# Moving the v copies to ACT, merging the substitution groups and changing two priorities in a scan-and-MLP kernel

## The chip, the cores and the metric

One core of a Trainium2 chip runs the whole program. The metric is device time in microseconds (us) of one launch; lower is better. A run is measured several times and the median is given.

## What is computed

The reference is a recurrence over 768 time steps (4 batches, 8 heads, head size 40) and then two MLPs over the 3072 resulting rows of 320 numbers:

```python
for t in range(S):
    y[:, :, t] = np.einsum('bhd,bhde->bhe', rt, state)
    Sa = np.einsum('bhde,bhe->bhd', state, at)
    state_decay = state * wt[:, :, None, :] - np.einsum('bhd,bhe->bhde', Sa, bt)
    state = state_decay + np.einsum('bhd,bhe->bhde', vt, kt)
...
h = x @ w_in                                    # 320 -> 2048
x = (np.maximum(h, 0) + alpha * np.minimum(h, 0)) @ w_out
g = x @ w_gate                                  # 320 -> 1536
out = (g / (1 + np.exp(-g)) * (x @ w_val)) @ w_out2
```

The weights come in as 64-bit floats and are narrowed on the chip.

## The kernel before, in words

**Blocks and items.** Time is cut into six blocks of 128 steps (`m` = 0 to 5), each of two chunks of 64. A block has four items, one for each batch, so there are 24. For each block the kernel does three things. `preps` builds, item by item, decay products by scans on DVE (`prep_a`, L502 and L509), the operand `AN` (L519), the operand `kbt` (L531), its products on PE (L543), copies of these on ACT into the block's triangular matrix `TT[m % 2]` (L549, L552) and into `AN` (L556, with a triangular select on POOL, L557), and transposed keys `KB` (L571, L574). `inverse(m)` inverts that matrix for all four items together. `seq` then carries the state through the two chunks of one item.

**The inverse.** The matrix is a 2x2 arrangement of 32x32 triangles. A DVE transpose (L589) brings the triangles into the scratch tile `ml`, and POOL writes an identity into `tl` (L591, L592). Then 31 substitution steps run on DVE: step `kk` multiplies the column `kk` of `ml` by the row `kk` of `tl` (L604) and subtracts the product from the rows below (L612). The columns of `tl` are cut into groups by `cuts`. For block 0 the cuts are 0, 16, 32 (`CL0`). For every later block they are 0, 10, 32 (`CUT`, `C2`); the second group has work only from step 10 on, and its columns do not depend on those of the first. Two DVE transposes (L615, L617) and two rounds of small matmuls with ACT copies (L625 to L652) finish the inverse. From block 1 on the scratch tiles share the two buffers of `kbt` (`scr`, L583), so the next block's `kbt` comes after the inverse has let go of them.

**The scan.** `seq(i, ch)` runs item `i` in chain 0 or 1; the two chains interleave. For each chunk `enter_chunk` takes one of two `gs` buffers: DVE writes the decayed state into one half of its partitions (L685, two instructions) and POOL decays the state itself (L685, POOL). Two POOL copies of 64 partitions by 160 elements put the rows of `v` in the other half (L699), after which `load_v` fetches the v of a later item. Then PE transposes the state (L707) and ACT copies it to `s0` (L709); PE multiplies (`zp`, L714), ACT copies (`zs`, L716), PE applies the inverse (`pp`, L724), ACT copies and negates (L726, L728, L734), PE forms `gp` (L741), DVE masks it (L744), PE forms `yp` (L756, L760), and DVE updates the state (L764) and scales the result (L768). The `yp` matmuls at L756 are the last readers of a `gs` buffer. The result goes to memory from ACT's queue (L776).

**The MLPs.** `mlp1(j)` runs block `j` of the first MLP in 16 steps `f`: 8 matmuls up (`up_mm`, L238), a leaky ReLU on ACT and DVE (L277, L278), a split into two parts (ACT L184, DVE L185), and 8 matmuls down. Its tiles take the places that the preparation of blocks 0 and 1 used, and its input is the scan's result. For block 0 its first eight steps run on the two halves of the batches one after the other. The second MLP runs at the end, after all scans.

**The conversion.** `conv1` narrows the first MLP's weights, 32 tiles in all: loads on SP's queue into two `raw` buffers, three DVE instructions (L172 to L174), one on ACT (L175), one more on DVE (L177), a copy on ACT (L184), a subtraction on POOL (L185), and a store on SP's queue.

**What sets the order.** The kernel is traced by `drive`, which advances several generators in proportion to their progress; each instruction gets a running number. A planner then orders each engine's queue: of the instructions that are ready it takes the one with the lowest number, and `drive` lowers the numbers of a generator by the amount given with it. While block 0 is scanned these amounts are as follows. `seq(0)`, `seq(1)`, and behind them `seq(2)` and `seq(3)`, have `SP` = 3000. `rest1`, which is the rest of block 1's preparation and then `inverse(1)`, has `HP2`. The conversion has `CP`. `mlp1(0)` has `MP` = 0. `CP` is also that of four conversions traced beside `inverse(0)`, which has 3000. From block 1 on scans, preparation and inverse all have 3000 and the MLP has 0. The conversion also carries an explicit edge (`behind`, L808): its DVE instructions come behind the latest step of the inverse that was traced before them. `rest1` is traced in 67 steps, 27 of preparation and 40 of `inverse(1)`, beside 26 conversions.

```python
drive(
    (seq(0, 0), N_SEQ, SP), (seq(1, 1), N_SEQ, SP),
    (take(rest1, int(nrest * RA)) if RA < 1 else rest1, FAC * nrest, HP2),
    (take(c1, NC1), NC1 - EC - EC0, CP),
)
```

Of the kernel before, what the change touches and what calls it, by code (L numbers as in the profile page):

```python
# [42 lines left out]
CL0 = (0, 16, 32)  # L43
# [1 line left out]
RA = 1.0  # L45
MP = 0
YB = 1
CP = 2000
HP2 = 3000
XI = 1  # L50
IB = 8
WB = 4
PRI = 3000
WCB = 2
GSB = 2
CUT = 0
C2 = 10
GPB = 2
DEP = 1
HOLD = 10  # L60
# [3 lines left out]
HALF = 32  # L64
# [4 lines left out]
def kernel(  # L69
# [15 lines left out]
    nc = tc.nc  # L85
# [34 lines left out]
    def drive(*gens, lead=0, engs=0, lag=1, who=0):  # L120
        live = [[*g, 0, j] for j, g in enumerate(gens)]
        names = ["PE", "DVE", "Activation", "Pool"]
        while live:
            e = min(live, key=lambda e: e[3] / e[1])
            try:
                tc.cur_priority -= e[2]
                with ExitStack() as st:
                    if e[4] >= lead and who >> (e[4] - lead) & 1:
                        for b in range(4):
                            log = crit.get(b, [])  # L130
                            if engs >> b & 1 and len(log) >= lag:
                                st.enter_context(tc.issue_after(log[-lag]))
                    n0 = len(traced())
                    ok = next(e[0], 0)
                    if e[4] < lead:
                        new = traced()[n0:]
                        for b in range(4):
                            mine = [x for x in new if str(x.engine).split(".")[-1] == names[b]]
                            if mine:
                                crit.setdefault(b, []).append(mine[-1])  # L140
                tc.cur_priority += e[2]
                e[3] += 1
                if ok == 0:
                    live.remove(e)
            except StopIteration:
                tc.cur_priority += e[2]
                live.remove(e)

    def chain(*gens):
        for g in gens:  # L150
            yield from g
# [427 lines left out]
    def scr(m, j):  # L579
        if m == 0:  # L580
            return bp.tile([128, HALF * HALF], F32, tag=f"la{j}", name="la")
        if ALIAS:
            return kbt_p.tile([128, HALF * HALF], F32, tag="kbt", name="la")  # L583
        return mac_p.tile([128, HALF * HALF], F32, tag=f"la{j}", name="la")

    def inverse(m):
        mc = tt = TT[m % 2]
        ml = scr(m, 0).rearrange("p (a b) -> p a b", a=HALF)
        nc.vector.transpose(out=ml, in_=mc[:, :, 0:HALF].rearrange("p n t -> p t n"))  # L589
        tl = scr(m, 1).rearrange("p (a b) -> p a b", a=HALF)  # L590
        nc.gpsimd.memset(tl, 0.0)  # L591
        nc.gpsimd.memset(tl.rearrange("p a b -> p (a b)")[:, 0:HALF * HALF:HALF + 1], 1.0)  # L592
        yield
        cuts = (CUT, C2, HALF) if m else CL0
        for kk in range(HALF - 1):
            tvs = []
            for c0, c1 in zip(cuts, cuts[1:]):
                nr, ns = HALF - 1 - kk, min(kk + 1, c1) - c0
                if ns <= 0:
                    continue  # L600
                most = max((HALF - 1 - q) * (min(q + 1, c1) - c0) for q in range(HALF))
                tmp = (mac_p if m else bp).tile([128, most], F32, tag=f"tmp{c0}", name="tmp")
                tv = tmp[:, 0:nr * ns].rearrange("p (a b) -> p a b", a=nr)
                nc.vector.tensor_tensor(  # L604
                    out=tv,
                    in0=ml[:, kk + 1:HALF, kk:kk + 1].to_broadcast([128, nr, ns]),
                    in1=tl[:, kk:kk + 1, c0:c0 + ns].to_broadcast([128, nr, ns]),
                    op=ALU.mult,
                )
                tvs.append((tv, tl[:, kk + 1:HALF, c0:c0 + ns]))  # L610
            for tv, dst in tvs:
                mark["inv"] = nc.vector.tensor_tensor(out=dst, in0=dst, in1=tv, op=ALU.subtract)  # L612
            yield
        tn = scr(m, 0).rearrange("p (a b) -> p a b", a=NG)
        nc.vector.transpose(out=tn.rearrange("p n s -> p s n"), in_=tl.rearrange("p t s -> p s t"))  # L615
        yield
        mark["inv"] = nc.vector.transpose(out=tt[:, :, 0:HALF].rearrange("p n t -> p t n"), in_=tl)  # L617
        yield
        es = scr(m, 1).rearrange("p (a b) -> p a b", a=NG)
        NH = NG // 2  # L620
        for g in range(2):
            eps = (ps_b if m else bps).tile([128, NH, HALF], F32, tag="b" if m else f"s{2 + g}", name="eps")
            for n in range(NH):
                for q in (0, 2):
                    nc.tensor.matmul(  # L625
                        eps[32 * q + 32:32 * q + 64, n, :],
                        mc[32 * q:32 * q + 32, g * NH + n, HALF:L],
                        tn[32 * q:32 * q + 32, g * NH + n, :],
                        tile_position=(32 * q, 32 * q + 32),
                    )  # L630
            for q in (1, 3):
                pr = slice(32 * q, 32 * q + 32)
                nc.scalar.copy(out=es[pr, g * NH:g * NH + NH], in_=eps[pr])
            yield
        for q in (1, 3):
            pr = slice(32 * q, 32 * q + 32)
            nc.scalar.copy(out=tt[pr, :, HALF:L], in_=tt[pr, :, 0:HALF])
            nc.gpsimd.memset(tt[pr, :, 0:HALF], 0.0)
            yield
        for g in range(2):  # L640
            dps = (ps_b if m else bps).tile([128, NH, HALF], F32, tag="b" if m else f"s{2 + g}", name="dps")
            for n in range(NH):
                for q in (1, 3):
                    nc.tensor.matmul(
                        dps[32 * q - 32:32 * q, n, :],
                        es[32 * q:32 * q + 32, g * NH + n, :],
                        tt[32 * q:32 * q + 32, g * NH + n, HALF:L],
                        tile_position=(32 * q, 32 * q - 32),
                    )
            for q in (0, 2):  # L650
                pr = slice(32 * q, 32 * q + 32)
                nc.scalar.mul(out=tt[pr, g * NH:g * NH + NH, HALF:L], in_=dps[pr], mul=-1.0)  # L652
            yield
# [7 lines left out]
    def seq(i, ch, own=None):  # L661
        m, bb = order[i]
# [32 lines left out]
        for c in range(CPB):  # L695
            cs = slice(c * L, c * L + L)
            gs = nxt
            for h, pr in ((0, hi), (1, lo)):
                nc.gpsimd.tensor_copy(  # L699
                    out=gs[pr, h::2, :, L:L + D],  # L700
                    in_=rv.rearrange("t (q j d) -> t q j d", j=2, d=D)[(lo, hi)[c], h::2],
                )
# [98 lines left out]
    def after(ins, g):  # L801
        while True:
            with tc.issue_after(ins.ins):
                if next(g, 0) == 0:
                    return
            yield

    def behind(g):  # L808
        while True:
            with tc.issue_after(mark["inv"].ins) if "inv" in mark else nullcontext():  # L810
                if next(g, 0) == 0:
                    return
            yield
# [10 lines left out]
    def take(g, n):  # L824
        for _ in range(n):
            if next(g, 0) == 0:
                return
            yield
# [8 lines left out]
    c1 = after(mark["prep"], c1)  # L837
    p1, c1 = behind(p1), behind(c1)
    drive((inverse(0), N_INV, HP), (take(p1, EP), EP + .1, BP), (take(c1, EC), EC + .1, CP), lead=1, engs=G0, lag=LG0, who=W0)
    p1, c1 = after(mark["inv"], p1), after(mark["inv"], c1)  # L840
    rest1 = chain(p1, inverse(1))
    nrest = B * N_PREP - EP + N_INV
    if FA == 0:
        drive(
            *((chain(seq(j, j), seq(j + 2, j)), 2 * N_SEQ, SP) for j in range(2)),
            (rest1, FAC * nrest, HP2),
            (take(c1, NC1), NC1 - EC - EC0, CP),
            lead=2, engs=G1, lag=LG1, who=W1,
        )
    else:  # L850
# [5 lines that stand above are left out]
# [9 lines left out]
    if FA:  # L865
        drive(
            (seq(2, 0), N_SEQ, SP), (seq(3, 1), N_SEQ, SP),
            (rest1, FAC * nrest * (1 - RA) + .1, HP2),
            (take(gms[0], 2 * FA + 1), 2 * FA + 1, MP),
        )  # L870
# [160 lines left out]
```

## Time and profile before

| what | value |
|---|---|
| median of 3 runs | 1250.2 us (1249.28 to 1252.76) |
| the profiled execution | 1245.15 us, its span 1243.4 us |
| mean granted TensorE clock in it | 0.949 of full speed |
| DVE / ACT / POOL busy | 781.3 us (63%) / 592.6 us (48%) / 312.6 us (25%) |
| end of `inverse(0)` and `inverse(1)`, last ACT instruction | 95.9 us, 205.9 us |
| last state update of the scans | 748 us |

All positions in the trace are in us from the start of the span. The profiled execution took 5 us less than the median of the runs, and 1.75 us of it lie outside its span. PE, PEld, DVE, ACT, POOL and SP are TensorE's matmuls, its weight loads, VectorE, ScalarE, GpSimd and the engine that issues most DMAs. Busy time is the union of an engine's instructions, so overlapping instructions are counted once; an instruction's duration runs from its start to its end even where the next one has started already.

### The profile page before, as it was taken

What the parts mean: (1) busy time and instruction counts of PE and PEld (TensorE: products, weight loads), DVE (VectorE), ACT (ScalarE), POOL (GpSimd) and SP (SyncE); (2) the same over time, 40 slices, a digit from 0 to 9 for tenths busy, and PEclk for the clock granted to TensorE, in tenths of its full rate; (3) what the DMA queues carried; (4) which work ended last, traced back from release to release, by engine and by line L of the source; (5) the groups of instructions that cost most, each with busy time, mean ns of one, the idle gap of its engine ahead of it and who ended that gap; (6) DMA issues with size and microseconds to landing.
All of it is one profiled execution on the core that took longest, in us unless ns stands there. A gap on an engine that the chain in (4) does not pass through costs nothing.

```text
span 1243.4 us, 24467 instructions
## 1 busy us (share of the span) xinstructions
PE 1095.8 (88%) x9056; PEld 928.7 (75%) x9056; DVE 781.3 (63%) x1689; ACT 592.6 (48%) x1463; POOL 312.6 (25%) x502
## 2 busy tenths in 40 slices
PE   3345787899799989989999899999999999999998
PEld 2244577777687777777777687888888888888887
DVE  7999999898669758974967444677732323232222
ACT  4547448844763674477455533455432323232222
POOL 9425443613121222252126300334500000000000
PEclk9658697999899999999999999999999999999999
DMA  5534577874545454464448648865210101000000
GB/s 149 168 115 133 180 257 251 263 228 126 161 127 176 134 161 142 144 196 145 145 139 266 201 131 292 283 213 153 73 47 1 47 1 38 1 22 1 22 1 22
DMA packets 92486, 166.36 MB, mean 134 GB/s; under 512 B 12752, under 2 KB 42704, under 8 KB 92368
## 3 DMA queue, kind: packets, MB, share of 16 engines
q1 hardware_dynamic: 84208, 160.87, 41.2%
q10 hardware_dynamic: 8160, 3.93, 1.1%
q8 instruction: 72, 1.18, 0.4%
q14 instruction: 46, 0.38, 0.1%
HBM read 136.98 MB, written 27.79 MB: 133 GB/s over the span
## 4 chain that ended last, share of the span: by engine, by line
PE 52%; DVE 20%; ACT 10%; DMA 8%; issue 6%; POOL 3%; SPq 1%; ACTq 0%; DVEq 0%; POOLq 0%
PE pg L238 10%; PE pv L238 10%; PE u L238 8%; PE o L952 3%; PE o L951 3%; PE o L953 3%; DVE la L612 3%; DVE tmp L604 3%; DMA raw_wa<-in_wa_dram 2%; PE gp L741 2%; PE d L243 2%; DMA xa<-xd 2%; PE d L244 2%; PE d L245 2%; DVE gs L685 2%
## 5 line engine op out<-in xcount | busy, mean ns | idle before, releaser
L184 ACT CAST gh<-g 128x512 fp32r<-128x512 f32 (+1 forms) x176 | 105.9, 602 | 175.2 <-DVE g L967 116.7
L967 DVE TENSOR_TENSOR g<-pv,sg 128x512 f32<-128x512 f32 x72 | 49.8, 691 | 200.1 <-PE pv L238 200.0
L185 DVE TENSOR_TENSOR gl<-g,gh 128x512 fp32r<-128x512 f32 (+1 forms) x176 | 119.5, 679 | 77.0 <-ACT gh L184 76.2
L238 PE MATMUL u<-xh,wt 128*128 128x512 f32 (+1 forms) x416 | 147.6, 397 | 15.9 <-DVE g L278 12.6
L278 DVE SCALAR_TENSOR_TENSOR g<-g,neg,u 128x512 f32<-128x512 f32 (+1 forms) x104 | 72.9, 701 | 63.0 <-ACT g L277 62.4
L238 PEld LDWEIGHTS u<-xh,wt 128*128 128x128 f32 x416 | 79.0, 193 | 34.9 <-DVE g L278 16.8
L238 PE MATMUL pg<-xh,w 128*128 128x512 f32 x288 | 102.0, 394 | 0.7 <-ACT sg L965 0.7
L965 ACT ACTIVATE sg<-pg 128x512 f32<-128x512 f32 x72 | 43.0, 597 | 124.3 <-PE pg L238 124.3
L238 PE MATMUL pv<-xh,w 128*128 128x512 f32 x288 | 100.5, 389 | 0.0
L277 ACT ACTIVATE g<-u 128x512 f32<-128x512 f32 (+1 forms) x104 | 58.7, 564 | 81.6 <-PE u L238 65.0
L543 PE MATMUL mnp<-AN,kbt 128*128 128x128 f32 x384 | 60.7, 311 | 32.1 <-POOL la L591 15.9
L952 PE MATMUL o<-w,gh 128*128 128x320 f32 x288 | 87.7, 309 | 0.0
L951 PE MATMUL o<-w,gh 128*128 128x320 f32 x288 | 87.1, 308 | 0.0
L244 PE MATMUL d<-gl,wt 128*128 128x512 f32 (+1 forms) x208 | 80.9, 391 | 1.2 <-DVE gl L185 1.2
L699 POOL COPY gs<-raw_v 64x160 f32<-64x160 f32 x96 | 42.3, 441 | 157.7 <-PE yp L756 70.1
L543 PEld LDWEIGHTS mnp<-AN,kbt 128*128 128x128 f32 x384 | 54.3, 219 | 36.2 <-POOL AN L517 17.6
L604 DVE TENSOR_TENSOR tmp<-la 128x96 f32<-128x96 f32 (+43 forms) x306 | 78.6, 281 | 3.2 <-POOL la L592 1.3
L238 PE MATMUL u<-xl,wt 128*128 128x512 f32 (+1 forms) x208 | 80.2, 386 | 0.2 <-DVE xl L185 0.2
L612 DVE TENSOR_TENSOR la<-la,tmp 128x96 f32<-128x96 f32 (+43 forms) x306 | 77.6, 278 | 1.9
L245 PE MATMUL d<-gh,wt 128*128 128x512 f32 (+1 forms) x208 | 78.5, 380 | 0.0
L557 POOL TENSOR_SCALAR_AFFINE_SELECT AN<-AN 64x256 f32<-64x256 f32 x96 | 48.5, 505 | 117.9 <-ACT AN L556 88.8
L953 PE MATMUL o<-w,gl 128*128 128x320 f32 x288 | 76.1, 309 | 0.0
(118 smaller groups left out, 2678.6 us busy)
## 6 DMA issues: line engine op xcount, KB each, us to landing
wt<-wd SPq DMA_DIRECT2D x98, 384.0 KB
wt<-wd SPq DMA_DIRECT2D x98, 320.0 KB
wd<-wc SPq DMA_DIRECT2D x24, 384.0 KB
raw<-in_moe_w_out_dram SPq DMA_DIRECT2D x28, 320.0 KB
raw_wa<-in_wa_dram SPq DMA_DIRECT2D x48, 160.0 KB
raw_bk<-in_bk_dram SPq DMA_DIRECT2D x48, 160.0 KB
wd<-wc SPq DMA_DIRECT2D x20, 320.0 KB
raw<-in_moe_w_in_dram SPq DMA_DIRECT2D x16, 256.0 KB
```

The costliest lines, as they stand in the source:

```text
L184: nc.scalar.copy(out=h, in_=raw)
L185: eng.tensor_tensor(out=l, in0=raw, in1=h.bitcast(F32), op=ALU.subtract)
L238: nc.tensor.matmul(ps, lt, rh, start=(i == 0), stop=(i == len(ops) - 1))
L244: nc.tensor.matmul(ps, wh, gl, start=False, stop=False)
L245: nc.tensor.matmul(ps, wl, gh, start=False, stop=last)
L278: nc.vector.scalar_tensor_tensor(g, g, neg[:, f:f + 1], ps, ALU.mult, ALU.add)
L543: nc.tensor.matmul(ps[:, s].rearrange("p h t -> p (h t)"), kbt[:, g * SH + s].rearrange("p j t -> p (j t)"), an[:, :, g * SH + s, :],)
L604: nc.vector.tensor_tensor(out=tv, in0=ml[:, kk + 1:HALF, kk:kk + 1].to_broadcast([128, nr, ns]), in1=tl[:, kk:kk + 1, c0:c0 + ns].to_broad ...
L612: mark["inv"] = nc.vector.tensor_tensor(out=dst, in0=dst, in1=tv, op=ALU.subtract)
L951: nc.tensor.matmul(ops[q], gh[:, ts], wh, start=first, stop=False)
L952: nc.tensor.matmul(ops[q], gh[:, ts], wl, start=False, stop=False)
L953: nc.tensor.matmul(ops[q], gl[:, ts], wh, start=False, stop=last)
```

## The change

The v copies go from `nc.gpsimd.tensor_copy` to `nc.scalar.copy`, with the same tiles and partitions. For blocks 1 to 5 the substitution has one group of columns instead of two. `CP` goes from 2000 to 3000 and `HP2` from 3000 to 1000.

```diff
-CP = 2000
-HP2 = 3000
+CP = 3000
+HP2 = 1000
...
-CUT = 0
-C2 = 10
...
-        cuts = (CUT, C2, HALF) if m else CL0
+        cuts = (0, HALF) if m else CL0
...
             for h, pr in ((0, hi), (1, lo)):
-                nc.gpsimd.tensor_copy(
+                nc.scalar.copy(
                     out=gs[pr, h::2, :, L:L + D],
                     in_=rv.rearrange("t (q j d) -> t q j d", j=2, d=D)[(lo, hi)[c], h::2],
                 )
```

## Rows read from the trace of the kernel before

**Rows 1.** The page's first part: busy time, share, instructions of PE.

```profile
PE 1095.8 (88%) x9056; PEld 928.7 (75%) x9056; DVE 781.3 (63%) x1689; ACT 592.6 (48%) x1463; POOL 312.6 (25%) x502
```

**Rows 2.** Busy time by stretch: length, PE, PEld, DVE, ACT, POOL, granted clock, DMA.

```profile
93.00:206.00 113.00, 81.25 (x997) 69.91 (x992) 106.35 (x270) 69.13 (x202) 48.96 (x76) 0.77 0.63 203
206.00:315.00 109.00, 97.27 (x1100) 83.83 (x1101) 96.36 (x235) 66.26 (x188) 39.97 (x68) 0.97 0.66 206
315.00:651.00 336.00, 307.90 (x3338) 252.50 (x3337) 246.16 (x614) 200.59 (x540) 88.73 (x168) 0.98 0.51 152
870.00:1243.00 373.00, 367.88 (x1905) 323.49 (x1903) 116.20 (x173) 104.98 (x187) 17.20 (x16) 1.00 0.07 23
```

**Rows 3.** The same view over the substitution of inverses 1 and 3.

```profile
118.00:191.00 73.00, 52.58 (x592) 44.85 (x594) 70.33 (x211) 33.95 (x105) 32.55 (x52) 0.79 0.66 213
...
357.00:413.00 56.00, 53.15 (x461) 42.18 (x461) 51.41 (x154) 23.35 (x62) 10.58 (x22) 1.00 0.53 158
```

**Rows 4.** Final transposes: inverse 1 (timeline of DVE), 2 and 3 (chain that ended last).

```profile
189.59 1.96 DVE L617 STREAM_TRANSPOSE tt<-la 128x1024 f32<-128x1024 f32 x1
...
299.56 2.00 DVE tt L617
...
411.16 1.99 DVE tt L617
```

**Rows 5.** Groups by line and form: substitution instructions of four sizes.

```profile
L612 DVE TENSOR_TENSOR la<-la,tmp 128x175 f32<-128x175 f32 x6 | 2.0, 333 | 0.0
...
L604 DVE TENSOR_TENSOR tmp<-la 128x10 f32<-128x10 f32 x5 | 0.8, 169 | 0.1
...
L604 DVE TENSOR_TENSOR tmp<-la 128x240 f32<-128x240 f32 x2 | 0.8, 399 | 0.0
...
L612 DVE TENSOR_TENSOR la<-la,tmp 128x63 f32<-128x63 f32 x2 | 0.4, 221 | 0.0
```

**Rows 6.** Timeline of DVE in inverse 0, two groups interleaved: start, length.

```profile
51.68 0.47 DVE L604 TENSOR_TENSOR tmp<-la 128x175 f32<-128x175 f32 x2
52.06 0.47 DVE L612 TENSOR_TENSOR la<-la,tmp 128x175 f32<-128x175 f32 x2
```

**Rows 7.** Timeline of DVE at the end of inverse 3, one group left.

```profile
407.16 0.19 DVE L604 TENSOR_TENSOR tmp<-la 128x30 f32<-128x30 f32 x1
407.38 0.19 DVE L612 TENSOR_TENSOR la<-la,tmp 128x30 f32<-128x30 f32 x1
```

**Rows 8.** The v copies: their group, their line, and who waited for them.

```profile
L699 POOL COPY gs<-raw_v 64x160 f32<-64x160 f32 x96 | 42.3, 441 | 157.7 <-PE yp L756 70.1 <-DVE tmp L604 46.6 <-DVE gl L185 17.3
...
L699 POOL COPY gs<-raw_v x96: 311/319/1166, 18.3 to 721.7; 64x160 f32<-64x160 f32 x96
...
  POOL wc L185: 1.0, 1
  PE sp L707: 0.3, 1
```

**Rows 9.** ACT copies by form: the same form from PSUM, a larger one from SBUF.

```profile
L734 ACT ACTIVATE gs<-pp 64x160 f32<-64x160 f32 x96 | 28.5, 297 | 5.4 <-PE pp L730 4.4
...
L676 ACT COPY pv<-raw_vt 128x256 f32<-128x256 f32 x48 | 17.2, 404 | 19.5 <-DMA xd<-pv 11.3 <-DMA raw_vt<-in_vt_dram 6.3 <-issue 1.6
```

**Rows 10.** Who waited: total us, times, longest; L764's wait; SP from 81 to 250.

```profile
POOL gs L699 <- PE yp L756: 70.1, 10, 20.2
...
  PE yp L760: 3.7, 5
...
SPq L210 <- POOL wc L185: 23.5, 12, 4.0
```

**Rows 11.** DVE readers of the raw weights (three for each conversion), 206 to 250 us: busy, instructions.

```profile
206.00:250.00 44.00, 13.57 (x21) 0.96 0.81 256
```

**Rows 12.** The conversion's fourth DVE instruction, by form.

```profile
L177 DVE SCALAR_TENSOR_TENSOR wz<-wz,wy 128x384 f32<-128x384 f32 x24 | 13.9, 580 | 4.2 <-ACT wz L175 3.9
```

## The prediction, made before the changed kernel had run

> **What bounds the kernel now.** I read the busy times first, then the stretches, then the parts that the change touches. PE is busy for 1095.8 of 1243.4 us [rows 1], so 148 us are PE's idle time, and only a smaller idle time (or a higher clock) can move the end: the matmuls themselves don't change. The stretches show where it lies [rows 2]. From 870 us on PE is idle for 5 of 373 us; nothing can be won there. From 93 to 206 it is idle for 32 of 113 us at a granted clock of 0.77, and DVE is busy for 106 of the 113: DVE binds. From 206 to 315 DVE has 96 of 109 us and PE 97: both bind. From 315 to 651 PE has 308 of 336 us (92%) and DVE 246 (73%): 28 us are left to win, and DVE time saved counts for about half, because PE is nearly full. I take that weight from these two shares; no row proves it.
>
> Within the later blocks DVE is again full while a substitution runs: 51.4 of 56 us in inverse 3 [rows 3], and inverses 2, 4 and 5 look the same. Preparation and inverse form a loop through the shared scratch buffers, and its period is steady: 299.56 to 411.16, 111.6 us between the last transposes of two inverses [rows 4].
>
> **One group instead of two, blocks 1 to 5.** Two groups take 31 + 21 = 52 pairs of instructions, one takes 31. So 42 instructions go from each inverse, 210 in all. The elements stay: the sum of (31 - kk)(kk + 1) over the steps is 5456 for each of the two lines. From 10 to 240 elements the duration grows from 169 to 399 ns, 1.0 ns an element, which leaves 159 ns fixed [rows 5]. But durations are not what DVE's time costs. In the interleaved groups a 175-element and a 63-element instruction last 333 + 221 = 554 ns [rows 5], while the next pair starts 0.38 us later [rows 6]: each starts some 85 ns before the one ahead ends. Where an instruction needs the result of the one just ahead, the start comes 0.22 us after a start of 0.19 us length [rows 7], 30 ns after its end. So the fixed part is about 75 ns when other work stands between, and 189 ns when not, 114 ns more.
>
> Before: 104 x 75 ns + 10.9 us of elements = 18.7 us, and 20 instructions of the last ten steps of the first group, which by then has no partner, at 114 ns more: 21.0 us. After: 62 x 75 ns + 10.9 = 15.6 us if other DVE work stands in every gap, 22.6 us if in none. The gain lies between 5.4 and -1.6 us for one inverse. Which end it is follows from how much other work there is: during inverse 1 DVE runs 211 instructions, 104 + 3 of them its own, so 104 others for 62 gaps [rows 3]; I take 5.0 us. During inverse 3 there are 154, so 47 others [rows 3], and they come in twos and threes; with 25 gaps filled, 37 x 114 ns remain and the gain is 1.2 us. Inverse 1 counts fully, inverse 2 nearly (1.0), the three later ones by half (1.8): **-7.8 us**.
>
> The rows contradict a rule that would make this part much larger. The Trainium skill (VectorE: DVE Perf Modes, The DRAIN you can't avoid) says that after each DVE instruction the next one waits until the pipeline has emptied, and that a semaphore between them adds nothing. By that rule each removed instruction gives back its whole fixed part; the starts in the rows contradict it for independent neighbours. What it would give is the second rival.
>
> **The copies.** POOL loses 96 x 441 ns = 42.3 us [rows 8]. Almost nothing waits for these copies: 1.0 us of a POOL instruction and 0.3 us of a transposition [rows 8]. So their going shortens no chain; the rest of the path from L764 to L709 (DVE, POOL's decay, PE) covers them, and it stays. What may be won is contention: the mean is 441 ns but the median 319 [rows 8], so something held the copies up for 96 x 122 ns = 11.7 us, and DVE may have been held as long. Between 0 and 11.7 us I take 4, a third of it before 315 us in full, two thirds by half: **-2.5 us**.
>
> ACT gains 96 copies of 64x160 from SBUF. The trace has that form only from PSUM, 297 ns, and a larger one from SBUF, 404 ns [rows 9]; I take 0.31 us, 30 us in all, 5 us a block of some 110. They must wait for the last reader of the `gs` buffer, `yp` at L756. POOL, with little else to do, waited 70.1 us for that; DVE, which waits for the end of the same group of matmuls at L764, 3.7 us [rows 10]. ACT is busy for 60% of the time from 93 to 651 [rows 2] and is like DVE in this; I take 3.7 us. Behind the waiting copies stand ACT's parts of the other chain, the MLP's ReLU and split, and the stores to memory at L776. For its own chain the copy lies where ACT has nothing to do. It delays others by 0.6 us a pair when ACT is busy: 48 x 0.6 x 0.6 = 17 us at worst, 0 at best, and as PE mostly has other matmuls queued I take 2.5 us net: **+2.5 us**. `load_v` on SP now follows ACT; its tile is for two items later, so nothing waits.
>
> **The priorities.** `inverse(1)` goes behind all four scans of block 0 and behind the conversion. The conversion can't run away from it: its edge holds it behind the inverse's steps, and by the proportional tracing 23 of the 26 conversions are traced before the substitution's last step. But it need no longer lag. Seven conversions run after 206 us now (21 readers in 13.57 us [rows 11], and 7 x about 0.55 us for the fourth instruction [rows 12]); less 28 overlaps of 85 ns that is 15 us of DVE. Three of the seven stay behind by the edge's count, so some 9 to 15 us of DVE work can come ahead of the end of inverse 1, and leave the stretch from 206 to 250, where DVE is nearly full. As long as DVE binds both stretches, order alone changes nothing: what inverse 1 loses the next block gets back. The scans of items 2 and 3 end earlier, so the second half of `mlp1(0)`'s input comes earlier, which can use some of PE's 32 idle us. Bounds: -6 (an estimate: a fifth of that idle time) and +15; I take **0**, the cover being that block 2's preparation and scan are freed of the same work. Without that cover it is the first rival. The conversion beside `inverse(0)` also rises, to the inverse's own priority: at most one more conversion, 2.2 us of DVE, falls inside; bounds 0 and +2.2, taken as 0 for the same reason. On SP's queue the conversions' loads and stores pass loads of block 1's raw tiles and weight fetches; their stores already held that queue for 23.5 us in 12 waits, 4.0 at most [rows 10]. Five more such waits early would be 10 us of SP's time, ahead of loads that are for an item or a step later; I take 0.
>
> **The sum.** -7.8 - 2.5 + 2.5 + 0 = -7.8 us. Against the profiled execution, 1245.15 us, that is 1237.3; that execution lies 5 us under the median of the runs, so for the median I say 1250.2 - 7.8 = **1242.4 us**.
>
> **Rivals.**
> - *Inverse 1 comes too late (slower).* For it: the loop's period was as long without conversions, 111.6 us [rows 4], as it was with seven of them (189.59 to 299.56, 110.0 [rows 4]), so freeing DVE of them may give nothing back. Price: at the upper bound all 15 us come before the end of inverse 1 and stay lost; less the 7.8, 1250.2 + 15 - 7.8 = 1257 us. It decides if the last transpose of inverse 1 ends after about 200 us and that of inverse 2 shifts as far. Against it: DVE was busy for 94% and 88% of the two stretches [rows 2], and in a full queue order gives back what it takes. 0.22.
> - *Every removed instruction counts (much faster).* With all gaps filled each inverse gains 5.4 us: 2 x 5.4 + 3 x 2.7 = 19 us, 1231 us. With the whole 159 ns for each of the 42 it is 6.7 us: 2 x 6.7 + 3 x 3.3 = 23 us, 1227 us. For it: the planner may put MLP work into each gap of the chain. Against it: 47 others for 62 gaps, and the starts of independent neighbours [rows 6]. 0.12 for the first and 0.08 for the second. The second is what the Trainium skill's rule above (VectorE: DVE Perf Modes, The DRAIN you can't avoid) would give.
> - *It does little.* One chain leaves its gaps open (-1.6 us each) and ACT's 5 us a block land where preparation needs ACT; together they eat the gain of inverse 1: about 1250 us. The priorities may also do less than they say, since the edge keeps the conversion's order. 0.13.
>
> My forecast has the remaining 0.45; its own range is 1237 to 1248.
>
> **How the numbers follow.** The measurement can tell some 0.3%, 3.8 us, from no change. Faster than 1246.4: 0.33 of the forecast, 0.20, 0.03 of the last case: 0.56. Within: 0.12 + 0.02 + 0.08 = 0.22. Slower than 1254: 0.20 of the first rival and 0.02: 0.22. The range goes from 1228, which leaves half of the case with the full fixed part outside, to 1258.
>
> **What would show it.** Right: 201 instead of 306 pairs on L604 and L612; the substitution of inverse 1 in about 17 us of DVE with other work in its gaps, the later ones one to two us shorter, with bare gaps of 30 ns; the ACT copies done before the `zp` matmuls without a wait of their own; fewer conversions after the end of inverse 1; PE's idle time before 315 us down by some 7 us. Wrong: inverse 1 ending past 200 us with the whole loop shifted; ACT standing for tens of us at L699 behind `yp`; or the gap between two blocks of the first MLP growing.

## The result, and the profile of the changed kernel

| | before | after |
|---|---|---|
| median, measured beside each other (13 runs each) | 1246.65 us (1239.98 to 1252.76) | 1254.82 us (1247.46 to 1260.1) |
| the profiled execution, its span | 1245.15, 1243.4 us | 1254.82, 1253.1 us |
| mean granted TensorE clock in it | 0.949 | 0.936 |
| PE busy, PE idle in the span | 1095.8, 147.6 us | 1104.7, 148.4 us |

The ratio of the times is 1.0067, with an interval of 1.0049 to 1.0086: slower by about 8 us. The time lies inside the predicted range, on the other side of no change than forecast. Lines of the changed kernel have numbers two lower (L612 is L610, L699 is L697).

First the page's busy times and PE's granted clock in 40 slices, of the changed kernel.

```profile
PE 1104.7 (88%) x9056; PEld 936.7 (75%) x9056; DVE 767.4 (61%) x1479; ACT 623.8 (50%) x1559; POOL 266.0 (21%) x406
...
PEclk9658695989899999999999899999999999999999
```

What was taken out of the engines is out: DVE has 210 instructions and 13.9 us less than in [rows 1], POOL 96 and 46.6 us less, and ACT has the 96 copies. Yet PE, whose instructions are the same 9056, is busy for 8.9 us longer, which is nearly the whole 9.7 us by which the span grew; its idle time is unchanged. (These are two single executions; the part on worse layouts below says how far that carries over to the other runs.) Next the stretches of [rows 2], and behind them the substitution of inverses 1 and 3 as in [rows 3] (columns: length; busy time of PE, PEld, DVE, ACT, POOL; granted clock; DMA share; GB/s).

```profile
93.00:206.00 113.00, 84.99 (x1003) 74.02 (x1003) 107.05 (x230) 73.66 (x218) 39.84 (x61) 0.77 0.66 212
206.00:315.00 109.00, 98.09 (x1045) 85.60 (x1047) 88.86 (x184) 71.12 (x201) 30.70 (x51) 0.89 0.63 194
315.00:651.00 336.00, 308.10 (x3261) 251.77 (x3256) 237.71 (x486) 213.63 (x584) 66.48 (x118) 0.97 0.50 151
870.00:1253.00 383.00, 377.36 (x1954) 331.53 (x1952) 125.52 (x187) 110.29 (x197) 22.22 (x21) 1.00 0.09 27
...
126.00:198.00 72.00, 56.03 (x618) 47.59 (x618) 69.78 (x163) 41.47 (x130) 23.82 (x38) 0.78 0.73 233
360.00:417.00 57.00, 54.64 (x416) 43.16 (x415) 50.29 (x113) 26.06 (x70) 6.62 (x14) 0.97 0.51 154
```

Between 206 and 315 us PE is busy for longer and gets fewer instructions done, 1045 for 1100, at 0.89 of the clock for 0.97. The two substitutions take as long as they did, though DVE runs 41 to 48 instructions fewer in each. The chain that ended last shows inverses 1 to 5 ending (start, length):

```profile
196.42 1.41 DVE tt L615
...
305.93 1.88 DVE tt L615
...
415.58 1.99 DVE tt L615
...
528.46 1.80 DVE tt L615
...
641.66 1.85 DVE tt L615
```

Inverse 1 comes 7 us late, and inverses 2 and 3 follow 6 and 4 us late ([rows 4] has 299.56 and 411.16). Cut at the ends of the inverses and at the last state update, the windows give this table. It tells where the 9.7 us are, and that it is PE's busy time that grows and shrinks with the length of a stage:

| stage up to | length | PE busy | clock |
|---|---|---|---|
| end of inverse 0 | 96.0 -> 98.0 | 33.5 -> 35.1 | 0.75 -> 0.70 |
| end of inverse 1 | 110.0 -> 119.0 | 81.0 -> 88.4 | 0.77 -> 0.75 |
| end of inverse 2 | 108.5 -> 102.0 | 96.8 -> 93.8 | 0.97 -> 0.94 |
| end of inverse 4 | 229.5 -> 229.5 | 208.2 -> 209.8 | 0.98 -> 0.96 |
| end of inverse 5 | 106.4 -> 112.5 | 99.7 -> 103.3 | 0.98 -> 1.00 |
| last state update | 97.6 -> 99.0 | 89.7 -> 90.3 | 0.98 -> 0.97 |
| end of the span | 495.4 -> 493.1 | 487.0 -> 484.0 | 1.00 -> 0.99 |

The copies and their waits, from the line's own view (durations: least, median, greatest; then what ended ACT's idle time ahead of them, and who waited for them):

```profile
L697 ACT COPY gs<-raw_v x96: 307/323/328, 4.4 to 730.9; 64x160 f32<-64x160 f32 x96
...
  PE yp L754: 11.6, 10
...
  ACT gs L697: 1.8, 1
  ACT wz L173: 0.4, 1
```

They cost 0.32 us each (forecast 0.31) and stood for 11.6 us behind `yp` (forecast 3.7), but hardly anything waited for them. The raw readers of conversions between 206 and 250 us (DVE, ACT):

```profile
206.00:250.00 44.00, 10.87 (x21) 3.65 (x7) 0.81 0.74 237
```

21 readers, as in [rows 11]: seven conversions still lie there. In time the new `CP` moved none of them ahead. Behind the end of inverse 1 there are fewer, 13 readers instead of 21, but only because that end came 11 us later. That the explicit edge kept the conversion's place is likely; no run took the edge away.

### The profile page after: what moved, and what is told of

It is laid out like the page before. It is cut to its first block, busy times and chain, and to the rows that moved or that the text cites. A ratio compares the mean times of both kernels' runs of the same rounds, so it can differ in the third digit from the quotient of the medians.

```text
span 1253.1 us, 24221 instructions
## 1 busy us (share of the span) xinstructions
PE 1104.7 (88%) x9056; PEld 936.7 (75%) x9056; DVE 767.4 (61%) x1479; ACT 623.8 (50%) x1559; POOL 266.0 (21%) x406
## 4 chain that ended last, share of the span: by engine, by line
PE 46%; DVE 14%; DMA 11%; ACT 9%; issue 4%; POOL 3%; SPq 1%; ACTq 0%; DVEq 0%; POOLq 0%
PE pg L236 9%; PE pv L236 9%; PE u L236 8%; PE o L951 3%; PE o L950 3%; PE o L949 3%; DMA xd<-pv 2%; DMA raw_wa<-in_wa_dram 2%; PE d L241 2%; PE d L242 2%; DMA wt<-wd 2%; PE d L243 1%; DVE la L610 1%; DVE tmp L602 1%; DMA raw_vt<-in_vt_dram 1%
## 5 line engine op out<-in xcount | busy, mean ns | idle before, releaser
L183 DVE TENSOR_TENSOR gl<-g,gh 128x512 fp32r<-128x512 f32 (+1 forms) x176 | 118.8, 675 | 81.2 <-ACT gh L182 79.4
L236 PE MATMUL u<-xh,wt 128*128 128x512 f32 (+1 forms) x416 | 150.7, 403 | 12.7 <-DVE g L276 6.1
L541 PE MATMUL mnp<-AN,kbt 128*128 128x128 f32 x384 | 63.8, 324 | 36.8 <-DVE AN L517 25.8
L541 PEld LDWEIGHTS mnp<-AN,kbt 128*128 128x128 f32 x384 | 57.9, 232 | 40.6 <-POOL AN L515 16.4
L243 PE MATMUL d<-gh,wt 128*128 128x512 f32 (+1 forms) x208 | 78.6, 380 | 0.0
L241 PE MATMUL d<-gh,wt 128*128 128x512 f32 (+1 forms) x208 | 70.1, 396 | 3.6 <-DMA wt<-wd 1.8
L183 POOL TENSOR_TENSOR wc<-wz,wc 128x384 fp32r<-128x384 f32 (+3 forms) x60 | 53.5, 903 | 92.1 <-ACT wc L182 47.4
L602 DVE TENSOR_TENSOR tmp<-la 128x31 f32<-128x31 f32 (+19 forms) x201 | 68.4, 345 | 4.1 <-POOL la L590 1.1
```

The lines of the kernel that those rows point to most:

```text
L183: eng.tensor_tensor(out=l, in0=raw, in1=h.bitcast(F32), op=ALU.subtract)
L236: nc.tensor.matmul(ps, lt, rh, start=(i == 0), stop=(i == len(ops) - 1))
L241: nc.tensor.matmul(ps, wh, gh, start=first, stop=False)
L243: nc.tensor.matmul(ps, wl, gh, start=False, stop=last)
L541: nc.tensor.matmul(ps[:, s].rearrange("p h t -> p (h t)"), kbt[:, g * SH + s].rearrange("p j t -> p (j t)"), an[:, :, g * SH + s, :],)
L602: nc.vector.tensor_tensor(out=tv, in0=ml[:, kk + 1:HALF, kk:kk + 1].to_broadcast([128, nr, ns]), in1=tl[:, kk:kk + 1, c0:c0 + ns].to_broad ...
```

## The experiments

The result leaves these theories open. **A**: the copies' load and waits on ACT cost more than the two other parts bring. **G**: one group leaves the chain's gaps open and costs time. **The late inverse**: the prediction's first rival. **D**: every part costs a little and the costs add up. A fifth came from the first runs: **the plan** (S). The planner lays out every queue anew after any edit, the layout of the kernel before is an unusually good one, and what an edit does has to be told from the loss of that layout. **Q**, formed later, tried to name what in the layout counts. Each ratio is to the kernel before, measured beside it on the same chip, with its 95% interval.

**Each part alone, and each pair.** The three parts are the hunks of the change's diff: the copies (`gpsimd.tensor_copy` to `scalar.copy`), the group (`cuts = (0, HALF)`), the priorities (`CP = 3000`, `HP2 = 1000`).

The copies alone:

> The kernel before with the v copies on ACT alone. Theory P (the priorities cost the time: inverse 1 ends at 217 instead of 206 us and the loop stays late): same as before, within 2 us of it. Theory A (30 us more on ACT delay preparation and scan): 5 to 9 us slower, the later inverses drifting apart by 1 to 3 us a block. Theory G (one group gives nothing and bares its gaps): same as before.

The group alone:

> The kernel before with one group of columns in blocks 1 to 5 alone. Theory P: same or up to 5 us faster, inverse 1 ending 3 to 5 us earlier. Theory A: the same as P. Theory G: 3 to 9 us slower, since the chain of 62 dependent instructions takes as long as 104 and lets lower work in between.

The priorities alone:

> The kernel before with the two priorities alone (CP 3000, HP2 1000). Theory P: 8 to 14 us slower, inverse 1 ending 10 to 15 us later than 206 and the end of inverse 2 later by at least 4. Theories A and G: within 3 us of before.

Copies and group, old priorities:

> Copies on ACT and one group, priorities as before. Theory P: same as before or up to 6 us faster. Theory A: 5 to 9 us slower than before. Theory G: 3 to 9 us slower. If A and G each hold a half, the sum of the two single runs.

Copies and priorities, two groups:

> Copies on ACT and the two priorities, two groups kept. Theory D (each part has a cost of its own that adds up: copies 29 us, one group 25, priorities 17 alone): far slower, 30 us or more. Theory L (any new plan of this kernel loses what the plan before had by luck or by tuning, once and not in proportion to what was changed): 5 to 30 us slower, no nearer to the sum than the others.

Group and priorities, copies on POOL:

> One group and the two priorities, copies kept on POOL. Theory D: 30 us or more slower than before. Theory L: 5 to 30 us slower. Theory M (the new priorities repair what one group and the copies break, the last steps of the first MLP's block 0 coming before 306 us again): about 5 to 12 us slower, like the whole change, with the last ReLU of block 0 of the MLP before 308 us.

| parts | ratio | median, us | inverse 1 ends |
|---|---|---|---|
| copies | 1.0237 (1.0218 to 1.0257) | 1274.3 | 205.3 |
| group | 1.0198 (1.0176 to 1.022) | 1269.25 | 207.0 |
| priorities | 1.0141 (1.0122 to 1.016) | 1260.21 | 219.1 |
| copies + group | 1.015 (1.0127 to 1.0174) | 1262.74 | 209.4 |
| copies + priorities | 1.0127 (1.0104 to 1.0149) | 1263.25 | 222.6 |
| group + priorities | 1.013 (1.0111 to 1.0149) | 1263.69 | 218.0 |
| all three | 1.0067 (1.0049 to 1.0086) | 1254.82 | 217.0 |

Every part alone costs two to three and a half times as much as the whole change, and the sum of the three would be 5.8%. So D falls, and A and G fall as sole causes: the group added to the copies makes them faster, and so do the copies added to group and priorities. As the one cause the late inverse falls too. In the two slowest kernels it ends at 205.3 and 207.0 us, within 1.1 us of before, and the four kernels in which it comes 11 to 17 us late have the four lowest ratios (of these the priorities, at 1.0141, and copies + group, at 1.015, can't be told apart). A share in the time it may have; see the part on worse layouts. The copies alone show it best: their scans end at 735.6 us, 12.6 us earlier than before, and the span is 28.7 us longer. Its page:

```profile
PE 1111.5 (87%) x9056; PEld 940.9 (74%) x9056; DVE 777.8 (61%) x1689; ACT 623.8 (49%) x1559; POOL 267.3 (21%) x406
```

15.7 of the 28.7 us are PE's busy time again. The copies wait 10.7 us in ten times behind `yp` here, less than the 11.6 us that they wait in the faster, changed kernel.

**A new layout without a change of the work.** `FAC` only sets at which pace a later block's preparation and inverse are numbered against the scans of the block before it; no instruction is added or removed. `C2` at 11 takes five pairs of instructions away.

```diff
-FAC = 1.0
+FAC = 1.02     # n_fac; 0.98 in nb_098, 1.04 in nb_104
...
-C2 = 10
+C2 = 11        # n_cut11 alone
```

> The kernel before with the second group starting at column 11 instead of 10: 51 instead of 52 pairs of instructions an inverse, no other work changed, but the planner lays out all the engines' queues anew. Theory L: 8 to 30 us slower, like the single parts. Theory D: within 3 us of before.

> The kernel before with the tracing proportion of preparation and inverse at 1.02 instead of 1.0 of their steps: no instruction changes, only the interleaving that the planner is given, by a fiftieth. Theory L: 5 to 30 us slower. Theory D: within 3 us of before.

> The kernel before with the tracing proportion at 0.98: no instruction changes, a new layout of the queues. Theory S (the plan of the kernel before is a picked one, and a new plan without any other change takes about 1.1% more): 0.7 to 2% slower than before. Theory W (the work that the change moves decides; the two shaken plans so far were unlucky): within 0.4% of before.

> The kernel before with the tracing proportion at 1.04. Theory S: 0.7 to 2% slower than before. Theory W: within 0.4% of before.

| kernel | ratio | span | PE busy | inverse 1 ends |
|---|---|---|---|---|
| C2 11 | 1.0135 (1.0112 to 1.0158) | 1262.3 | 1114.0 | 205.7 |
| FAC 1.02 | 1.0095 (1.0073 to 1.0117) | 1257.0 | 1103.6 | 207.8 |
| FAC 0.98 | 1.0115 (1.0083 to 1.0147) | 1256.4 | 1110.2 | 207.1 |
| FAC 1.04 | 1.011 (1.0083 to 1.0137) | 1261.6 | 1107.4 | 209.4 |

All four are slower than the kernel before and have higher ratios than the changed kernel (FAC 1.02 within the two intervals); the mean is 1.0114, 14 us. Nothing in them costs 14 us by itself: three have the very same instructions. The page of the one with FAC at 1.04:

```profile
PE 1107.4 (88%) x9056; PEld 940.9 (75%) x9056; DVE 782.5 (62%) x1689; ACT 593.3 (47%) x1463; POOL 314.2 (25%) x502
```

DVE, ACT and POOL are within 2 us of [rows 1]; PE is up by 11.6. What differs is the order. The traces have 9056 matmuls each; with two of them matched by line and tile names as far as one common order goes, 785 stand elsewhere than before at FAC 1.02, 1199 at 0.98, 1154 at 1.04 and 934 in the changed kernel. So a price of about 1.1% for a new layout is shown, and it is larger than the effect that was to be measured.

**What makes the layout good: the first MLP's block 0?** Sorted by span, the first nine kernels fell in two heaps: where the MLP's first block was done late against the scans' hand-over, spans were 18.9 to 29.2 us longer than before, otherwise 9.7 to 14.8. Q says that this sets the time. Three runs lifted block 0 of the MLP in the order:

```diff
-g.append((take(gm, nm - held), nm, 0))
+g.append((take(gm, nm - held), nm, 3300 if m == 1 else 0))   # 2500 in m_copies_behind
```

The copies alone, lifted by 3300 and by 2500, and the whole change, lifted by 3300:

> The copies on ACT alone, as in the run that was 2.4% slower, and the first MLP's steps of block 0 lifted by 3300 while block 1 is scanned: in ACT's queue the last ReLU of MLP block 0 then stands ahead of the end of inverse 2 (place 383 against 399) where it stood behind it (410 against 389). Theory Q (whether MLP block 0 is through before the hand-over between two blocks is what costs 10 to 20 us): 0.7 to 1.4% slower than before. Theory A (ACT's extra 30 us are the loss): still 2% or more slower.

> The same with a lift of 2500: the queues are laid out anew as much, but the last ReLU stays behind the end of inverse 2 (place 408 against 400). Theory Q: 1.5 to 2.5% slower than before, and slower than the run with 3300. Theory A: 2% or more slower. If only chance rules (theory L without a place that decides), no order between the two runs.

> The changed kernel with the same lift of 3300: the last ReLU of MLP block 0, already ahead of the end of inverse 2 (place 388 against 396), goes to place 373 against 399. Theory Q: no further gain, within 0.5% of the changed kernel. If being earlier always pays: faster than the changed kernel by 5 us or more, perhaps faster than the kernel before.

The block's last ReLU came at 299.6, 320.6 and 296.0 us (303.7 in the kernel before), so the lift did what it should. The ratios were 1.0121 (1.0099 to 1.0142), 1.0095 (1.0065 to 1.0125) and 1.0197 (1.0172 to 1.0221). The later block went with the faster of the two kernels, and the earliest of all with one of the slowest. Q falls. The two runs with the copies say one more thing: the copies, at 1.0237 alone, came to 1.0121 and 1.0095 in other layouts, where kernels without them stand. So ACT's 31 us are no cost that shows, as far as these two go: they lift the MLP too, and no run lifted it in the kernel before. The third run is a fifth layout of the whole change, and at 1.0197 one of the slowest kernels.

**The change in new layouts.** The same shake, now of the whole change, and of copies and group without the priorities; the edit is FAC alone, 0.98, 1.02 or 1.04.

> The changed kernel with the tracing proportion at 1.02 instead of 1.0, nothing else: the counterpart, on this side, of the run that took 0.95% more. The place of the last ReLU stays ahead. Theory L: the changed kernel is not a special plan, so this run takes about the same, 0.5 to 1.5% more than before. If the changed kernel is a picked plan like the one before, 0.8% more than the changed kernel or worse.

> The changed kernel with the tracing proportion at 0.98. Theory S: 0.3 to 1.5% slower than before, that is about as the changed kernel (0.7%) and its first shaken plan (0.5%); the change's own work is then worth the difference of the two families' means, some -0.5%. Theory W: 0.5 to 0.9% slower, always the same.

> The changed kernel with the tracing proportion at 1.04. Theory S: 0.3 to 1.5% slower than before. Theory W: 0.5 to 0.9% slower.

> Copies on ACT and one group with the old priorities, tracing proportion 0.98 (at 1.0 this took 1.5% more than before). Theory S1 (the half per cent that the change is worth comes from the DVE work saved, as predicted, and the priorities are worth nothing): 0.4 to 0.9% slower than before, like the family of the changed kernel. Theory S2 (it comes from the priorities): 1.0 to 2.0% slower.

> The same with the tracing proportion at 1.02. Theory S1: 0.4 to 0.9% slower than before. Theory S2: 1.0 to 2.0% slower.

| | FAC 0.98 | 1.0 | 1.02 | 1.04 | mean |
|---|---|---|---|---|---|
| kernel before | 1.0115 | 1 | 1.0095 | 1.011 | 1.0107 without 1.0 |
| copies + group | 1.011 (1.0077 to 1.0142) | 1.015 | 1.0203 (1.0165 to 1.0242) | | 1.0154 |
| whole change | 1.0075 (1.0046 to 1.0105) | 1.0067 | 1.0048 (1.0025 to 1.0072) | 1.0055 (1.0035 to 1.0076) | 1.0061 |

With the run of C2 the four new layouts of before have the mean 1.0114. The four of the whole change lie together, 1.0048 to 1.0075, all below the lowest of those four: by the means of these FAC layouts the change gives back 0.53%, 6.6 us. This holds for this one kind of shake. With the MLP lifted, the whole change took 1.0197; with that fifth layout its mean is 1.0088 and its layouts spread over 1.5%, so that a worth of the change from layout to layout is no longer shown. Copies and group without the priorities give nothing back under FAC, 1.011 to 1.0203. The page of the fastest profiled one (FAC 1.04):

```profile
PE 1103.0 (88%) x9056; PEld 936.7 (75%) x9056; DVE 770.1 (62%) x1479; ACT 625.6 (50%) x1559; POOL 266.1 (21%) x406
```

Its inverse 1 ends at 218.1 us, as late as in the changed kernel. No version that ran beat the kernel before.

**Where the time goes in a worse layout.** Over all 19 other profiles the span is longer than in the one of before by 17.6 us in the mean, and PE's busy time by 14.4, 82% of it. The rows show how matmuls get longer. Windows of the changed kernel, around one such place:

```profile
376.00:386.00 10.00, 7.64 (x70) 5.30 (x68) 8.28 (x19) 4.45 (x12) 0.78 (x2) 1.00 0.66 210
386.00:390.00 4.00, 4.00 (x24) 2.88 (x22) 3.27 (x7) 2.38 (x7) 0.00 (x0) 0.57 0.46 141
390.00:400.00 10.00, 10.00 (x80) 8.33 (x80) 8.51 (x20) 5.49 (x15) 0.00 (x0) 1.00 0.55 163
```

The granted clock falls to 0.57 for 4 us, about the lower of its two levels, 1.2 of 2.4 GHz. The timeline of PE says what came before (start, length, idle time ahead and what ended it):

```profile
385.85 0.66 PE L712 MATMUL zp<-gs,AN 128*64 128x40 f32 x16 [2.00 <-ACT s L707]
...
388.32 0.63 PE L236 MATMUL u<-xl,wt 128*128 128x512 f32 x1
388.74 0.63 PE L236 MATMUL u<-xh,wt 128*128 128x512 f32 x1
```

PE had stood for 2.00 us until ACT's copy of the state arrived, and the matmuls of the first MLP then start 0.42 us apart. The kernel before, at the same work and the same place, stood for 0.66 us only, and they start 0.22 us apart:

```profile
388.29 0.39 PE L238 MATMUL u<-xl,wt 128*128 128x512 f32 x1
388.51 0.39 PE L238 MATMUL u<-xh,wt 128*128 128x512 f32 x1
```

In the profiles of before, of the changed kernel and of FAC 1.02, each of the 22 falls of the clock after 206 us (the last microseconds of the span apart) comes in or just after a stand of PE of 1.2 us or more, and lasts 3.4 to 10.2 us. Eight of these stands are at `zp`, more than at any other place; the view of waits (total, times, longest) has, after

```profile
PE zp L712 <- ACT s L707: 20.7, 13, 4.2
```

and before

```profile
PE zp L714 <- ACT s L709: 15.5, 8, 4.8
```

Not every stand is followed by a fall: 17 of 1.2 us or more in the three traces are not. In the kernel before PE stood here as long as in the place above, and the clock stayed (timeline of PE, then a window):

```profile
437.85 0.66 PE L714 MATMUL zp<-gs,AN 128*64 128x40 f32 x16 [2.02 <-ACT s L709]
...
438.00:450.00 12.00, 11.46 (x102) 9.72 (x101) 5.26 (x8) 9.92 (x32) 1.63 (x4) 1.00 0.60 174
```

What the clock costs can be summed from the traces. PE is busy at the lower level for 79.9 us before and 97.2 after; at the higher level the 17.3 us more would take half as long, so the clock accounts for 8.7 of the 8.9 us. Over the 19 other profiles it is 25.2 us more in the mean, worth 12.6 of the 14.4 us. In the changed kernel most of it, 11.9 us, lies between 206 and 230 us, around the end of its late inverse 1 (the window before, then after):

```profile
206.00:230.00 24.00, 20.87 (x193) 18.54 (x193) 22.06 (x38) 20.36 (x64) 13.97 (x21) 1.00 0.76 236
...
206.00:230.00 24.00, 18.89 (x157) 17.03 (x157) 20.04 (x34) 16.46 (x48) 7.38 (x10) 0.65 0.67 208
```

All this compares with one execution of the kernel before, and that one had a high clock: 0.949, where its 56 runs beside the experiments had 0.944 in the mean (0.935 to 0.950) and the changed kernel's 13 runs 0.937. An estimate from these clocks has PE at the lower level for 140 us before and 159 after, 19 us more and not the 33 of the two profiles. The 18 kernels of the experiments have 21 us more in the mean, and take 16.1 us more. If three quarters of the 21 us find PE busy, as in the profiles (25.2 of 33.7), the clock explains 8 of the 16 us, about half. Nor does it rank the kernels: before at FAC 0.98 and the whole change at FAC 1.02 each have 18 us more at the lower level than before, and took 1.0115 and 1.0048. So matmuls at the lower level are a large part of what a worse layout costs; the rest was not located, and no run forced or removed one single stand.

## Why the prediction was wrong

**The step that failed.** The sum puts the order of the queues at nothing: "order alone changes nothing", priorities **0**, and all terms added to the kernel before as it stood. The runs show that order alone is worth more than the whole forecast: with the very same instructions, FAC at 0.98, 1.02 and 1.04 cost 0.95 to 1.15%, 12 to 14 us. The largest term of the sum, -7.8 for one group, was mis-sized besides, at inverse 1. And the sum started from 1250.2, the median of three runs; beside the changed kernel the one before took 1246.65, so that a forecast of -7.8 stands against +8.2.

**One group, -7.8.** Over the whole kernel the instructions went as said: the mean of one on the first of the two lines (L604, now L602) rose from 281 to 345 ns, where 71 elements more (5456 over 31 instead of 52) at 1.0 ns make 71. The length of a substitution did not follow. From the start of L589 to the end of the last transpose (L617 before), inverses 1 to 5 took 73.6, 58.2, 56.2, 56.1 and 48.6 us, and then 72.4, 55.2, 57.1, 56.9 and 47.3. Forecast was -5.0 for inverse 1 and -1.2 for each later one; measured are -1.2, -2.9, +0.9, +0.8, -1.3. The bounds given for one inverse, a gain of 5.4 and a loss of 1.6, hold for all five. In the run of the group alone the five took 76.7, 57.0, 56.7, 55.8 and 50.4 us, so the other two parts hide no gain. Nearer to the forecast is the DVE time of the substitution's own instructions, from each start to the next with idle time (gaps beyond 60 ns) left out. In the later inverses it fell from 22.7, 21.7, 21.4 and 22.5 us to 21.6, 20.9, 20.7 and 21.6; they have 30 to 37 bare gaps of 61, where 37 of 62 were assumed, so there the size of the term was roughly right. What failed is the 5.0 for inverse 1: 22.9 us before and 22.6 after, where 21.0 and 16.0 were forecast. Its gaps were filled as assumed (10 of 61 bare), but the instructions got slower than their size says. DVE's groups by line, in the window of the substitution of inverse 1, before (118 to 191 us):

```profile
L612 DVE TENSOR_TENSOR la<-la,tmp 128x40 f32<-128x40 f32 (+37 forms) x52 | 15.1, 306 | 0.1
L604 DVE TENSOR_TENSOR tmp<-la 128x40 f32<-128x40 f32 (+37 forms) x52 | 13.8, 283 | 0.1
...
L685 DVE TENSOR_TENSOR gs<-ST,Wx 64x160 f32<-64x160 f32 x14 | 4.7, 336 | 0.1
```

and after (126 to 198 us):

```profile
L610 DVE TENSOR_TENSOR la<-la,tmp 128x31 f32<-128x31 f32 (+15 forms) x31 | 13.1, 421 | 0.3
L602 DVE TENSOR_TENSOR tmp<-la 128x31 f32<-128x31 f32 (+15 forms) x31 | 12.6, 406 | 0.2
...
L683 DVE TENSOR_TENSOR gs<-ST,Wx 64x160 f32<-64x160 f32 x12 | 5.2, 437 | 0.1
```

With 71 ns more for the elements the two lines should take 377 and 354 ns; they take 44 and 52 ns more, 3.0 us over 31 pairs, and the state's decay (L683), whose form did not change, takes 101 ns more. What they ran beside says more. Against 159 ns and 1.0 ns an element, the estimate from [rows 5], the 62 instructions together take 4.9 us too long, and 4.4 of that falls on the 12 of them that overlap POOL's subtraction of the conversion (L183, in the last section). Before it was 3.2 us for 104, 2.9 of it on the 29 beside the same POOL line. In the four later inverses of the changed kernel none runs beside it, and the excess is 0.4 to 0.6 us each. This is a coincidence in time, in every inverse; no run took the POOL line away. Nor is it all: without the excess the two substitutions would have 19.7 and 17.7 us of DVE time, a gain of 2.0 and still not 5.0.

The Trainium skill (VectorE: DVE Perf Modes, The DRAIN you can't avoid) adds to its rule that a next instruction that is not held starts earlier; the prediction left that out. The trace agrees with the addition for independent neighbours: in the last fence below one starts at 154.57 us, 80 ns before the one ahead ends. So the rows contradict the rule only as the prediction put it.

**Copies, -2.5 and +2.5.** The duration was right, the wait was 11.6 and not 3.7 us, and it cost nothing that shows (copies in other layouts 1.0095 and 1.0121, with the MLP lifted, against 1.0114 without copies). What DVE's instructions beside the copies took over the least of their form came to 7.5 us before and is gone with the copies; 4 were taken, which by the weights given makes 2.7 and not 2.5.

**Priorities, 0.** Half right in their parts, wrong in what they do: the conversion moved not at all in time, inverse 1 ends 11 us later, and still, in the FAC layouts, the priorities are the part without which the other two bring nothing. "As long as DVE binds both stretches, order alone changes nothing" is the step that the runs refute most plainly, since with one and the same work FAC alone moves the time by 1%.

**The missing term.** The sum was made against the kernel before as if its order were a given, to which small costs are added. About +14 us for a new layout, less the 6.6 us of the FAC layouts, is +7.6 us, and +8.2 was measured. That the two agree proves nothing, since the changed kernel is one of the four behind the 6.6; and that 6.6 is near the forecast 7.8 is no success of the terms, because they were not found at their places and the fifth layout does not show it. No row of the kernel before shows this price; only another layout of the same kernel does.

**"Only a smaller idle time (or a higher clock) can move the end".** True, and the bracket was then forgotten: between the two profiles idle time went from 147.6 to 148.4 us and the clock made the difference. The mean clocks of the other runs differ by about half as much.

**The rival "inverse 1 comes too late"** named the right sign and a time of 1257, and part of its place came true (last transpose at 198.4 us, inverse 2 six us later). But its deciding point does not decide: each kernel with the new priorities has inverse 1 ending at 217 to 225 us, and the four FAC layouts of the whole change, the fastest after the kernel before, are among them. The price was there in part, in a form that the rival did not name: the low clock between 206 and 230 us.

**Left open.** Which stands the layout of before avoids, and by which neighbours in the queues, was not found; holding every queue's order fixed while one cost changes was not tried. `CP` and `HP2` were not tried apart, so which of them is worth the 0.5% of the FAC layouts is open, and so are why it needs the other two parts and why the lifted MLP undoes it.

## What to carry to other kernels

Where a planner lays the queues out, a good time can be that of a good layout: here four new layouts with the same or nearly the same work all cost about 1.1%, and none of 19 other kernels was as fast. (That the kernel before had been kept as the best of many layouts would explain it; nothing here shows it.) An edit gives such luck up and must be worth more, or be laid out as often. Compare families, not single kernels: shake a parameter that changes no work, in both versions, and set mean against mean; and take more than one kind of shake. And read PE's busy time and granted clock beside its idle time, in several runs: a stand of 2 us can be paid twice.

## What the runs showed of the hardware that was not expected

A DVE instruction can be held up for most of a microsecond beside one of POOL. Timeline of the changed kernel, DVE and POOL around 154 us (start, length):

```profile
154.17 0.48 DVE L171 SCALAR_TENSOR_TENSOR wz<-raw,wy 128x320 uint32<-128x320 uint32 x1
154.57 1.22 DVE L610 TENSOR_TENSOR la<-la,tmp 128x252 f32<-128x252 f32 x1
155.72 0.41 DVE L183 TENSOR_TENSOR xl<-xa,xh 128x256 fp32r<-128x256 f32 x1
...
154.50 1.02 POOL L183 TENSOR_TENSOR wc<-wz,wc 128x384 fp32r<-128x384 f32 x1 [5.34 <-ACT wc L182]
```

The 252-element subtraction takes 1.22 us while POOL's subtraction of the conversion runs; its neighbours of about the same size take 0.41. At 167.33 the same pair meets again, 1.23 us. Put each DVE instruction to the POOL instruction that it overlaps longest, and take from it the least duration of its line and form. Beside this POOL line (84 instructions) the excess sums to 37.7 us over 146 DVE instructions, and to 36.3 over 158 before; beside the 96 copies it was 7.5 over 145, and without any POOL instruction alongside 21.6 over 1095 (both before). That is 0.26, 0.23, 0.05 and 0.02 us each. POOL's decay of the state (L683) has two inputs as well and comes to 0.05 only, so two inputs alone do not make the difference. To move the copies was to move the smaller of the two.
